# The first group of a fused dynamic-convolution and gated-MLP kernel: its down products taken in three fp32r parts instead of one float32 product

## The chip, the cores and the metric

One core of one Trainium2 chip. The time is the device time of one execution in microseconds (us); the kernel before was run three times, and its median is 1341.92 us (1340.8 to 1342.03). In the profile, PE is TensorE's matmul, PEld its weight load, DVE is VectorE, ACT ScalarE, POOL GpSimd, SP the queue that issues the DMAs.

## What is computed

```python
w = softmax(weight_gen, axis=-1)                # [4, 4096, 8, 7]
x = sum over k of w[:, s, h, k] * x_pad[:, s + k, h, :]   # causal, 7 taps, [4, 4096, 192]
x = x.reshape(16384, 192)
g = x @ w_gate                                  # [16384, 1536]
silu = g * (1 / (1 + exp(-g)))
out = (silu * (x @ w_val)) @ w_out              # [16384, 192]
```

x and weight_gen are float32, the three matrices are float64 in memory; the result is float32.

## The kernel before, in words

The 16384 tokens are worked in 32 groups g of 512 (JG = 4 tiles of 128). For each group the hidden width of 1536 is worked in 12 steps f of 128, so there are 384 steps, numbered i = 12 g + f. A value is held as a pair: hi is the value rounded to fp32r, lo the rest, and a product a b is taken as three fp32r products, hi hi, lo hi and hi lo.

A step of TensorE has three kinds of work. `up_first` (L440 for the left 64 rows of the width, L443) and `up_second` (L452) take the products with w_gate and w_val into two PSUM banks, in halves of 64 rows; four banks rotate, so the banks of step i are needed again at step i + 2 and come free when DVE has read them. `down` (L497, L504, L513) multiplies the gated value of the step two before (LAG = 2) with w_out and sums over f. Between the two halves of a sum stands a marker: `told` puts an empty instruction into POOL's queue that waits for the first half, and `behind` lets the second half wait for this instruction. So TensorE's `up_second` waits until POOL's queue has come as far as the marker of its step (the releaser is shown as POOLq L281).

After `up_second`, ACT takes `silu` of the gate (sg, L460), and `gated` multiplies it with the value on DVE. In groups 1 to 31 this gives h (L474), its rounded part hi on ACT (L475), then one other piece of DVE work, then lo (L477). In group 0 (PLAIN = 1) all other pieces of the step come first, and then one product, hi, in plain float32 (L469); it has no lo.

The weights come as float64 and are made float32 while group 0 runs. For each f four pieces (`weight_ops`) do this: `exponent` (DVE e L363, ACT Relu L372 and Sign L374, POOL sign L375), `mantissa_high` (DVE m L380), `mantissa_low` (DVE m L390), and `value32` (DVE w L403, then the splits of the first two matrices: hi on ACT L353, lo on POOL L354). Step i of group 0 holds value32 of f = i + 2, mantissa_high of i + 3, exponent of i + 4 and mantissa_low of i + 3, in this order, and behind them pieces of the softmax and of the convolution of group 1 (DVE prod L231, xatt L261; three products aside on POOL, L231). The part of w_out is copied into a float32 tile `wo32` (ACT L417), which the down product of group 0 reads in float32 (L497). In steps 9 to 13 (WO = 9) the twelve parts of `wo32` are split into `wo` hi and lo (ACT L353, POOL L354), for groups 1 to 31.

Every engine works its instructions in the order in which this program writes them.

Of the kernel before, what the change touches and what calls it, by code (L numbers as in the profile page):

```python
# [8 lines left out]
F32 = mybir.dt.float32  # L9
F32R = mybir.dt.float32r  # L10
I32 = mybir.dt.int32
AF = mybir.ActivationFunctionType
ALU = mybir.AluOpType
# [5 lines left out]
def dynconv_glu_kernel(  # L19
# [23 lines left out]
    nc = tc.nc  # L43
    B, S, D = x.shape
# [3 lines left out]
    P = 128  # L48
# [6 lines left out]
    NF = F // P  # L55

    LAG = 2
# [1 line left out]
    LEAD1 = 1  # L59
    EXP1 = 16  # L60
    LOAD1 = 1
    WO = 9

    PLAIN = 1

    HELPED = (3, 3)
    ASIDE = max(HELPED)
# [6 lines left out]
    const = ctx.enter_context(tc.tile_pool(name="const", bufs=1))  # L74
# [15 lines left out]
    wb_hi = const.tile([P, F], F32R, name="wb_hi")  # L90
    wb_lo = const.tile([P, F], F32R, name="wb_lo")
    wo = const.tile([P, NF, 2, D], F32R, name="wo")
    wo32 = const.tile([P, NF, D], F32, name="wo32")

    xr = x.rearrange("b (q t) d -> (b q) t d", t=T)
    wgr = weight_gen.rearrange("b (q t) h k -> (b q) t (h k)", t=T)
# [182 lines left out]
    def told(ins):  # L279

        nop = nc.gpsimd.nop()  # L281
        tc.add_manual_dep(nop.ins, ins.ins.name, SYNC, reason="the sum's other half")
        return nop
# [51 lines left out]
    NW = 3 * P + D  # L335
    raw_t = {}

    def load_weights(f):
        raw = stage.tile([P, NW, 2], I32, tag="raw", name="raw", bufs=RAW)
        fs = slice(f * P, (f + 1) * P)  # L340
        pieces = (
            (raw[:, 0:P], w_gate[0:P, fs]),
            (raw[:, P : 2 * P], w_val[0:P, fs]),
            (raw[0:DB, 2 * P : 3 * P], w_gate[P:D, fs]),
            (raw[DB:P, 2 * P : 3 * P], w_val[P:D, fs]),
            (raw[:, 3 * P : NW], w_out[fs]),
        )
        for dst, src in pieces:
            nc.sync.dma_start(out=dst.rearrange("p n w -> p (n w)"), in_=src.bitcast(I32))  # L349
        raw_t[f] = raw  # L350

    def split(hi, lo, src):
        nc.scalar.activation(out=hi, in_=src, func=AF.Copy)  # L353
        nc.gpsimd.tensor_tensor(out=lo, in0=src, in1=hi.bitcast(F32), op=ALU.subtract)  # L354

    def weight_ops(f):
        st = {}
        fs = slice(f * P, (f + 1) * P)

        def exponent():  # L360
            raw = st["raw"] = raw_t.pop(f)
            e = stage.tile([P, NW], I32, tag="e", name="e")
            nc.vector.tensor_scalar(  # L363
                out=e,
                in0=raw[:, :, 1],
                scalar1=20,
                scalar2=0x7FF,
                op0=ALU.logical_shift_right,
                op1=ALU.bitwise_and,
            )  # L370

            nc.scalar.activation(out=e, in_=e, func=AF.Relu, scale=TWO23, bias=exp_bias)  # L372
            sign = stage.tile([P, NW], F32, tag="sign", name="sign")
            nc.scalar.activation(out=sign, in_=raw[:, :, 1], func=AF.Sign)  # L374
            nc.gpsimd.tensor_tensor(out=sign, in0=sign, in1=e.bitcast(F32), op=ALU.mult)  # L375
            st["scale"] = sign

        def mantissa_high():
            st["m"] = stage.tile([P, NW], I32, tag="m", name="m")
            nc.vector.tensor_scalar(  # L380
                out=st["m"],
                in0=st["raw"][:, :, 1],
                scalar1=0xFFFFF,
                scalar2=4,
                op0=ALU.bitwise_and,
                op1=ALU.logical_shift_left,
            )

        def mantissa_low():
            nc.vector.scalar_tensor_tensor(  # L390
                out=st["m"],
                in0=st["raw"][:, :, 0],
                scalar=28,
                in1=st["m"],
                op0=ALU.logical_shift_right,
                op1=ALU.bitwise_or,
            )
            if f + RAW < NF:
                load_weights(f + RAW)

        def value32():
            w = stage.tile([P, NW], F32, tag="w", name="w")
            nc.vector.scalar_tensor_tensor(  # L403
                out=w,
                in0=st["m"],
                scalar=float(2**24),
                in1=st["scale"],
                op0=ALU.add,
                op1=ALU.mult,
            )  # L410
            split(wb_hi[:, fs], wb_lo[:, fs], w[:, 2 * P : 3 * P])
            split(
                wa_hi[:, :, fs],
                wa_lo[:, :, fs],
                w[:, 0 : 2 * P].rearrange("p (i n) -> p i n", i=2),
            )
            nc.scalar.activation(out=wo32[:, f], in_=w[:, 3 * P : NW], func=AF.Copy)  # L417

        return [exponent, mantissa_high, mantissa_low, value32]


    h_t = {}
    acc = {}
# [38 lines left out]

    def gated(g, f, sums, sg, between):
        hi = hp.tile([P, NC], F32R, tag="hi", name="hi", bufs=KEEP)
        if g < PLAIN:
            while between():
                pass
            h = hi.bitcast(F32)
            nc.vector.tensor_tensor(out=h, in0=sums[1], in1=sg, op=ALU.mult)  # L469
            h_t[g, f] = h, None  # L470
            return
        h = hp.tile([P, NC], F32, tag="h", name="h")
        lo = hp.tile([P, NC], F32R, tag="lo", name="lo", bufs=KEEP)
        nc.vector.tensor_tensor(out=h, in0=sums[1], in1=sg, op=ALU.mult)  # L474
        nc.scalar.activation(out=hi, in_=h, func=AF.Copy)  # L475
        between()
        nc.vector.tensor_tensor(out=lo, in0=h, in1=hi.bitcast(F32), op=ALU.subtract)  # L477
        h_t[g, f] = hi, lo
# [5 lines left out]
    def down(g, f, pair, second):  # L484


        hi, lo = h_t[g, f]
        opens, closes = f == 0 and not second, f == NF - 1 and second
        ts = (2 * pair, 2 * pair + 1)
        if opens:  # L490
            for t in ts:
                acc[t] = ps_dn.tile([P, 2 * D], F32, tag=f"dn{t}", name=f"dn{t}")
        order = ts if (f + second) % 2 == 0 else ts[::-1]
        tiles = [(t, r, slice(t * P, (t + 1) * P)) for t, r in zip(order, (LOW, HIGH))]
        if lo is None:
            made = [
                nc.tensor.matmul(  # L497
                    acc[t][:, 0:D], hi[r, cs], wo32[r, f], start=opens, stop=closes
                )
                for t, r, cs in tiles  # L500
            ]
        else:
            made = [
                nc.tensor.matmul(  # L504
                    acc[t],
                    hi[r, cs],
                    wo[r, f].rearrange("p a d -> p (a d)"),
                    start=opens,
                    stop=False,
                )  # L510
                for t, r, cs in tiles
            ] + [
                nc.tensor.matmul(  # L513
                    acc[t][:, 0:D], lo[r, cs], wo[r, f, 0], start=False, stop=closes
                )
                for t, r, cs in tiles
            ]
        if not second:
            half_done[pair] = told(made[-1])
            return  # L520
        behind(made[0], half_done.pop(pair))
        if f < NF - 1:
            return
        if pair == 0:
            osb_t[g] = outp.tile([P, JG, 2 * D], F32, tag="osb", name="osb", bufs=1)
        osb = osb_t[g]
        n = D if lo is None else 2 * D
        for t in ts:
            nc.scalar.activation(out=osb[:, t, 0:n], in_=acc[t][:, 0:n], func=AF.Copy)
        if g < NG - 1 and pair == 0:  # L530
            return
        t0, t1 = (ts[0] if g == NG - 1 else 0), ts[1] + 1
        if lo is not None:
            a = osb[:, t0:t1]
            nc.vector.tensor_tensor(
                out=a[:, :, 0:D], in0=a[:, :, 0:D], in1=a[:, :, D:], op=ALU.add
            )
        nc.sync.dma_start(
            out=outr[:, g * JG + t0 : g * JG + t1], in_=osb[:, t0:t1, 0:D]
        )  # L540
# [6 lines left out]
    def spread(ops, first, last):  # L547

        for n, op in enumerate(ops):
            at = first + (n * (last - first)) // len(ops)  # L550
            todo.setdefault(max(at, 0), []).append(op)

    with tc.manual_schedule():
# [31 lines left out]
        for i in range(NF):  # L585
# [4 lines left out]
        todo[0] += later[:3]  # L590
        spread(loads, LOAD1, LOAD1 + 7)
        spread(later[3:], NF - LEAD - 2, NF - LEAD)
        spread(
            [lambda f=f: split(wo[:, f, 0], wo[:, f, 1], wo32[:, f]) for f in range(NF)],
            WO,
            NF + LAG - 1,
        )
        for c in range(1, len(wcuts)):
            s0 = (wcuts[c - 1][0] // JG - 1) * NF - LEAD if c > 1 else NF
            s1 = (wcuts[c][0] // JG - 1) * NF - LEAD  # L600
# [18 lines left out]
        for i in range(len(steps) + LAG + 1):  # L619
            ops = todo.pop(i, [])  # L620
            to_turn = turned.get(i)
            if i < len(steps):
                g, f = steps[i]
                sums, nop = up_first(g, f)
# [19 lines left out]
            if i < len(steps):  # L644
                up_second(g, f, sums, nop)
                sg = silu(sums)
# [6 lines left out]
            if i < len(steps):  # L653

                def between():
                    if ops:
                        ops.pop(0)()
                    return ops
# [40 lines left out]
```

## Time and profile before

| | |
|---|---|
| median of three runs | 1341.92 us |
| the profiled execution | 1342.55 us, span of its instructions 1340.8 us |
| TensorE busy | 1287.4 us, 96% |
| DVE busy | 1010.5 us, 75% |
| ACT busy | 608.5 us, 45% |
| POOL busy | 71.8 us, 5%, all of it before 108 us |
| mean granted clock of TensorE | 0.991 |

The span runs from the first to the last instruction. Busy time of an engine counts its instructions, not its waits; a matmul's end is modelled. Group 0 lasts from the first up product at 30.78 us to about 103 us.

### The profile page before, as it was taken

To read this page: it belongs to the slowest core of one execution; us is meant where nothing else is said; L and a number is where in the kernel's file an instruction comes from. 1 tells how busy PE (TensorE), PEld (TensorE's weight loads), DVE (VectorE), ACT (ScalarE), POOL (GpSimd) and SP (SyncE) were. 2 spreads that over 40 slices of the span, in tenths; PEclk is the share of its full clock that TensorE was granted. 3 is DMA by queue.
4 is the path that set the end of the run, shared out by engine and by line. 5 is a ranking of instruction groups with operands and counts; after the bars stand their busy time and mean duration, and the time that the engine had idled before them with its cause. 6 is when DMAs were issued, how large, how long until landed. Compare 5 with 4: busy or idle time off the path is not lost.

```text
span 1340.8 us, 31630 instructions
## 1 busy us (share of the span) xinstructions
PE 1287.4 (96%) x13560; PEld 1205.6 (90%) x13560; DVE 1010.5 (75%) x1385; ACT 608.5 (45%) x1073; POOL 71.8 (5%) x66
## 2 busy tenths in 40 slices
PE   1689999999999999999999999999999999999998
PEld 0578999999999999999999999999999999999998
DVE  8988787777877777887777788777778777777753
ACT  3445444454444445444444544444454444444443
POOL 6761000000000000000000000000000000000000
PEclk9879999999999999999999999999999999999999
DMA  5421100101110010110101011010101001000000
GB/s 152 140 75 34 55 13 13 43 13 55 33 55 13 2 55 13 54 34 23 41 4 55 13 54 31 13 43 13 55 13 55 14 1 54 13 13 13 13 14 13
DMA packets 28580, 47.36 MB, mean 35 GB/s; under 512 B 2076, under 2 KB 25628, under 8 KB 26648
## 3 DMA queue, kind: packets, MB, share of 16 engines
q1 hardware_dynamic: 28440, 45.34, 10.5%
q8 instruction: 106, 1.74, 0.5%
q14 instruction: 34, 0.28, 0.1%
HBM read 32.75 MB, written 12.58 MB: 34 GB/s over the span
## 4 chain that ended last, share of the span: by engine, by line
PE 88%; DVE 5%; ACT 3%; DMA 2%; issue 1%; SPq 1%; POOL 0%; ACTq 0%; DVEq 0%; POOLq 0%
PE dn L504 22%; PE up L440 21%; PE up L452 20%; PE up L443 18%; PE dn L513 5%; PE tr L300 1%; DVE h L474 1%; DMA xt<-in_x_dram 1%; SPq L349 1%; ACT sg L460 1%; DVE xatt L261 1%; DMA raw<-in_moe_w_gate_dram 1%; DVE m L390 1%; ACT wt L183 0%; ACT L460 0%
## 5 line engine op out<-in xcount | busy, mean ns | idle before, releaser
L504 PE MATMUL dn<-wo,hi 64*128 64x384 f32 x2976 | 599.6, 346 | 0.4 <-ACT hi L475 0.4
L513 PE MATMUL dn<-wo,lo 64*128 64x192 f32 x2976 | 531.7, 248 | 0.3 <-DVE lo L477 0.3
L504 PEld LDWEIGHTS dn<-wo,hi 64*128 64x128 f32 x2976 | 476.2, 184 | 19.0 <-ACT hi L475 0.6
L513 PEld LDWEIGHTS dn<-wo,lo 64*128 64x128 f32 x2976 | 443.3, 186 | 9.0 <-DVE lo L477 0.5
L474 DVE TENSOR_TENSOR h<-up,sg 128x512 f32<-128x512 f32 x372 | 256.8, 690 | 240.4 <-ACT sg L460 240.3
L460 ACT ACTIVATE sg<-up 128x512 f32<-128x512 f32 x384 | 229.4, 597 | 381.3 <-PE up L452 347.0
L475 ACT ACTIVATE hi<-h 128x512 fp32r<-128x512 f32 x372 | 235.2, 632 | 298.1 <-DVE h L474 298.1
L477 DVE TENSOR_TENSOR lo<-h,hi 128x512 fp32r<-128x512 f32 x372 | 255.5, 687 | 73.2 <-ACT hi L475 73.2
L440 PE MATMUL up<-xhi,wb_hi 64*128 64x512 f32 x768 | 242.4, 424 | 5.3 <-DVE hi L469 3.4
L452 PE MATMUL up<-xhi,wa_hi 64*128 64x512 f32 x768 | 234.2, 426 | 11.5 <-POOLq L281 11.4
L440 PE MATMUL up<-xlo,wb_hi 64*128 64x512 f32 x768 | 229.2, 394 | 0.9 <-DVE xlo L325 0.9
L440 PE MATMUL up<-xhi,wb_lo 64*128 64x512 f32 x768 | 229.0, 395 | 0.0
L443 PE MATMUL up<-xhi,wa_hi 64*128 64x512 f32 x768 | 227.6, 392 | 0.0
L443 PE MATMUL up<-xhi,wa_lo 64*128 64x512 f32 x768 | 227.6, 392 | 0.0
L443 PE MATMUL up<-xlo,wa_hi 64*128 64x512 f32 x768 | 226.7, 390 | 0.0
L452 PE MATMUL up<-xhi,wa_lo 64*128 64x512 f32 x768 | 220.3, 392 | 0.0
L452 PE MATMUL up<-xlo,wa_hi 64*128 64x512 f32 x768 | 219.5, 390 | 0.0
L231 DVE TENSOR_TENSOR prod<-xt,wt 128x768 f32<-128x768 f32 x186 | 181.9, 978 | 0.2
L261 DVE TENSOR_TENSOR xatt<-xatt,prod 128x768 f32<-128x768 f32 x186 | 179.1, 963 | 0.0
L440 PEld LDWEIGHTS up<-xhi,wb_hi 64*128 64x128 f32 x768 | 136.9, 185 | 11.6 <-DVE hi L469 4.5
L443 PEld LDWEIGHTS up<-xhi,wa_hi 64*128 64x128 f32 x768 | 137.0, 186 | 9.3
L443 PEld LDWEIGHTS up<-xhi,wa_lo 64*128 64x128 f32 x768 | 136.6, 185 | 9.1
(57 smaller groups left out, 1354.6 us busy)
## 6 DMA issues: line engine op xcount, KB each, us to landing
xt<-in_x_dram SPq DMA_DIRECT2D x14, 1344.0 KB, 5.6
out_dram<-osb SPq DMA_DIRECT2D x31, 384.0 KB, 2.6
raw<-in_moe_w_out_dram SPq DMA_DIRECT2D x12, 192.0 KB, 2.8
wt<-in_weight_gen_dram SPq DMA_DIRECT2D x3, 672.0 KB, 4.0
raw<-in_moe_w_gate_dram SPq DMA_DIRECT2D x12, 128.0 KB, 2.1
raw<-in_moe_w_val_dram SPq DMA_DIRECT2D x12, 128.0 KB, 2.3
wt<-in_weight_gen_dram SPq DMA_DIRECT2D x4, 224.0 KB, 4.4
xt<-in_x_dram SPq DMA_DIRECT2D x2, 384.0 KB, 4.5
```

The costliest lines, as they stand in the source:

```text
L231: engine.tensor_tensor(out=into.rearrange("p t (h i) -> p t h i", h=H), in0=src, in1=w, op=ALU.mult)
L261: nc.vector.tensor_tensor(out=a, in0=a, in1=tmp.pop(k), op=ALU.add)
L300: nc.tensor.transpose(ps[half][:, t * P + r.start : t * P + r.stop], xatt[g][r, t, half * P : (half + 1) * P], ident[r, r],)
L440: nc.tensor.matmul(ps, w[r, fs], m[r], start=(n == 0), stop=False)
L443: ins = nc.tensor.matmul(sums[i], w[r, i, fs], m[r], start=False, stop=False)
L452: ins = nc.tensor.matmul(sums[i], w[r, i, fs], m[r], start=False, stop=(n == len(full) - 1))
L460: nc.scalar.activation(out=sg, in_=sums[0], func=AF.Silu)
L474: nc.vector.tensor_tensor(out=h, in0=sums[1], in1=sg, op=ALU.mult)
L475: nc.scalar.activation(out=hi, in_=h, func=AF.Copy)
L477: nc.vector.tensor_tensor(out=lo, in0=h, in1=hi.bitcast(F32), op=ALU.subtract)
L504: nc.tensor.matmul(acc[t], hi[r, cs], wo[r, f].rearrange("p a d -> p (a d)"), start=opens, stop=False,)
L513: nc.tensor.matmul(acc[t][:, 0:D], lo[r, cs], wo[r, f, 0], start=False, stop=closes)
```

## The change

PLAIN is gone: group 0 takes the same way as the others, with h, hi and lo, and three down products. `value32` splits its part of w_out at once into `wo` hi and lo; the tile `wo32` and the twelve later splits are gone. The closing addition of the two halves of a sum is now done for group 0 too.

```diff
-            nc.scalar.activation(out=wo32[:, f], in_=w[:, 3 * P : NW], func=AF.Copy)
+            split(wo[:, f, 0], wo[:, f, 1], w[:, 3 * P : NW])
...
     def gated(g, f, sums, sg, between):
         hi = hp.tile([P, NC], F32R, tag="hi", name="hi", bufs=KEEP)
-        if g < PLAIN:
-            while between():
-                pass
-            h = hi.bitcast(F32)
-            nc.vector.tensor_tensor(out=h, in0=sums[1], in1=sg, op=ALU.mult)
-            h_t[g, f] = h, None
-            return
         h = hp.tile([P, NC], F32, tag="h", name="h")
...
-        if lo is None:
-            made = [
-                nc.tensor.matmul(
-                    acc[t][:, 0:D], hi[r, cs], wo32[r, f], start=opens, stop=closes
-                )
-                for t, r, cs in tiles
-            ]
-        else:
-            made = [
...
-        spread(
-            [lambda f=f: split(wo[:, f, 0], wo[:, f, 1], wo32[:, f]) for f in range(NF)],
-            WO,
-            NF + LAG - 1,
-        )
```

DVE, steps 1 and 2 of the program, the kernel before (e and the first m are the pieces of the exponent and the high mantissa, the second m the low one, w the float32 weight, hi the gated product of the step):

```order
L403 SCALAR_TENSOR_TENSOR w<-m,sign 128x576
L380 TENSOR_SCALAR m<-raw 128x576
L363 TENSOR_SCALAR e<-raw 128x576
L390 SCALAR_TENSOR_TENSOR m<-raw,m 128x576
L231 TENSOR_TENSOR prod<-xt,wt 128x768
L469 TENSOR_TENSOR hi<-up,sg 128x512
L403 SCALAR_TENSOR_TENSOR w<-m,sign 128x576
L380 TENSOR_SCALAR m<-raw 128x576
L363 TENSOR_SCALAR e<-raw 128x576
L390 SCALAR_TENSOR_TENSOR m<-raw,m 128x576
L261 TENSOR_TENSOR xatt<-xatt,prod 128x4x192
L469 TENSOR_TENSOR hi<-up,sg 128x512
```

and the same two steps of the changed kernel:

```order
L463 TENSOR_TENSOR h<-up,sg 128x512
L399 SCALAR_TENSOR_TENSOR w<-m,sign 128x576
L466 TENSOR_TENSOR lo<-h,hi 128x512
L376 TENSOR_SCALAR m<-raw 128x576
L359 TENSOR_SCALAR e<-raw 128x576
L386 SCALAR_TENSOR_TENSOR m<-raw,m 128x576
L227 TENSOR_TENSOR prod<-xt,wt 128x768
L463 TENSOR_TENSOR h<-up,sg 128x512
L399 SCALAR_TENSOR_TENSOR w<-m,sign 128x576
L466 TENSOR_TENSOR lo<-h,hi 128x512
```

The gated product has moved from the end of its step to its head, and lo stands between w and the masks.

ACT, step 1, before:

```order
L460 ACTIVATE sg<-up 128x512
L353 ACTIVATE wb_hi<-w 128x128
L353 ACTIVATE wa_hi<-w 128x2x128
L417 ACTIVATE wo_93<-w 128x192
L372 ACTIVATE e<-e,exp_bias 128x576
L374 ACTIVATE sign<-raw 128x576
```

and now:

```order
L456 ACTIVATE sg<-up 128x512
L464 ACTIVATE hi<-h 128x512
L349 ACTIVATE wb_hi<-w 128x128
L349 ACTIVATE wa_hi<-w 128x2x128
L349 ACTIVATE wo<-w 128x192
L368 ACTIVATE e<-e,exp_bias 128x576
L370 ACTIVATE sign<-raw 128x576
```

The rounding of h stands between the Silu and the conversions; the copy of w_out's part is the first half of its split now.

POOL, steps 1 and 2, before (sign is the product of sign and scale):

```order
L354 TENSOR_TENSOR wb_lo<-w,wb_hi 128x128
L354 TENSOR_TENSOR wa_lo<-w,wa_hi 128x2x128
L375 TENSOR_TENSOR sign<-sign,e 128x576
L354 TENSOR_TENSOR wb_lo<-w,wb_hi 128x128
L354 TENSOR_TENSOR wa_lo<-w,wa_hi 128x2x128
L375 TENSOR_TENSOR sign<-sign,e 128x576
L231 TENSOR_TENSOR aside<-xt,wt 128x768
```

and now:

```order
L350 TENSOR_TENSOR wb_lo<-w,wb_hi 128x128
L350 TENSOR_TENSOR wa_lo<-w,wa_hi 128x2x128
L350 TENSOR_TENSOR wo<-w,wo 128x192
L371 TENSOR_TENSOR sign<-sign,e 128x576
L350 TENSOR_TENSOR wb_lo<-w,wb_hi 128x128
L350 TENSOR_TENSOR wa_lo<-w,wa_hi 128x2x128
L350 TENSOR_TENSOR wo<-w,wo 128x192
L371 TENSOR_TENSOR sign<-sign,e 128x576
L227 TENSOR_TENSOR aside<-xt,wt 128x768
```

Each step has a third split, ahead of the sign product and the marker behind it.

## Rows read from the trace of the kernel before

**Rows 1.** The page of the profile: busy time of each engine with its share and instructions; then, over the span in 40 slices, the busy share of DVE and TensorE's granted clock, in tenths.
```profile
PE 1287.4 (96%) x13560; PEld 1205.6 (90%) x13560; DVE 1010.5 (75%) x1385; ACT 608.5 (45%) x1073; POOL 71.8 (5%) x66
DVE  8988787777877777887777788777778777777753
PEclk9879999999999999999999999999999999999999
```

**Rows 2.** Busy time by stage: the stretch, its length, then for PE, PEld, DVE, ACT and POOL the busy us and the instructions in brackets, TensorE's granted clock, the share of the DMA engines, GB/s.
```profile
45.00:50.00 5.00, 1.67 (x8) 1.39 (x10) 5.00 (x5) 1.39 (x2) 4.89 (x4) 0.68 0.19 57
50.00:55.00 5.00, 5.00 (x36) 4.39 (x36) 5.00 (x7) 2.80 (x6) 3.68 (x4) 0.64 0.83 273
55.00:60.00 5.00, 3.26 (x34) 2.68 (x34) 5.00 (x5) 2.74 (x6) 3.95 (x5) 1.00 0.35 108
60.00:65.00 5.00, 3.93 (x38) 3.25 (x40) 5.00 (x7) 2.79 (x6) 3.85 (x4) 1.00 0.57 163
...
95.00:100.00 5.00, 5.00 (x54) 4.76 (x52) 4.03 (x5) 2.67 (x8) 3.54 (x4) 1.00 0.00 0
```

**Rows 3.** Timeline of DVE: start in us, duration in us, engine, line, operation, out<-in and shapes, count, and in square brackets the idle time before it and what ended it.
```profile
32.35 0.45 DVE L380 TENSOR_SCALAR m<-raw 128x576 int32<-128x576 int32 x1
...
35.13 0.76 DVE L403 SCALAR_TENSOR_TENSOR w<-m,sign 128x576 f32<-128x576 int32 x1 [1.30 <-POOL sign L375]
...
41.63 0.68 DVE L469 TENSOR_TENSOR hi<-up,sg 128x512 f32<-128x512 f32 x1
...
57.48 0.71 DVE L363 TENSOR_SCALAR e<-raw 128x576 int32<-128x576 int32 x1
...
60.18 0.68 DVE L469 TENSOR_TENSOR hi<-up,sg 128x512 f32<-128x512 f32 x1
60.78 1.38 DVE L403 SCALAR_TENSOR_TENSOR w<-m,sign 128x576 f32<-128x576 int32 x1
62.08 0.45 DVE L380 TENSOR_SCALAR m<-raw 128x576 int32<-128x576 int32 x1
62.45 0.45 DVE L363 TENSOR_SCALAR e<-raw 128x576 int32<-128x576 int32 x1
...
77.37 0.74 DVE L403 SCALAR_TENSOR_TENSOR w<-m,sign 128x576 f32<-128x576 int32 x1
78.04 1.68 DVE L380 TENSOR_SCALAR m<-raw 128x576 int32<-128x576 int32 x1
...
87.14 0.68 DVE L469 TENSOR_TENSOR hi<-up,sg 128x512 f32<-128x512 f32 x1
...
90.67 0.69 DVE L469 TENSOR_TENSOR hi<-up,sg 128x512 f32<-128x512 f32 x1 [0.45 <-ACT sg L460]
```

**Rows 4.** Timeline of POOL, the same columns.
```profile
59.82 1.73 POOL L375 TENSOR_TENSOR sign<-sign,e 128x576 f32<-128x576 f32 x1 [1.05 <-ACT sign L374]
62.58 0.63 POOL L354 TENSOR_TENSOR wb_lo<-w,wb_hi 128x128 fp32r<-128x128 f32 x1 [1.04 <-PE up L443]
63.18 1.24 POOL L354 TENSOR_TENSOR wa_lo<-w,wa_hi 128x256 fp32r<-128x256 f32 x1
...
92.88 1.70 POOL L354 TENSOR_TENSOR wo<-wo,wo 128x192 fp32r<-128x192 f32 x3
```

**Rows 5.** Timeline of TensorE (matmuls), the same columns: the second parts of four steps of group 0, its first and third pair, and of two steps of group 1.
```profile
48.33 0.79 PE L452 MATMUL up<-xhi,wa_hi 64*128 64x512 f32 x2 [3.99 <-POOLq L281]
...
49.34 0.63 PE L452 MATMUL up<-xhi,wa_lo 64*128 64x512 f32 x2
...
59.88 0.50 PE L452 MATMUL up<-xhi,wa_hi 64*128 64x512 f32 x2 [1.74 <-POOLq L281]
...
60.44 0.40 PE L452 MATMUL up<-xhi,wa_lo 64*128 64x512 f32 x2
...
97.64 0.53 PE L452 MATMUL up<-xhi,wa_hi 64*128 64x512 f32 x1
...
101.00 0.52 PE L452 MATMUL up<-xhi,wa_hi 64*128 64x512 f32 x1
...
152.02 0.41 PE L452 MATMUL up<-xhi,wa_hi 64*128 64x512 f32 x1
...
155.22 0.41 PE L452 MATMUL up<-xhi,wa_hi 64*128 64x512 f32 x1
```

**Rows 6.** Timeline of ACT, the same columns: the Silu of steps 0 and 4, and the two instructions that lead to POOL's sign product.
```profile
36.76 0.60 ACT L460 ACTIVATE sg<-up 128x512 f32<-128x512 f32 x1 [3.42 <-PE up L452]
...
58.28 0.77 ACT L372 ACTIVATE e<-e,exp_bias 128x576 int32<-128x576 int32 x1 [1.38 <-DVE e L363]
58.97 0.70 ACT L374 ACTIVATE sign<-raw 128x576 f32<-128x576 int32 x1
60.94 0.60 ACT L460 ACTIVATE sg<-up 128x512 f32<-128x512 f32 x1 [1.27 <-PE up L452]
```

**Rows 7.** Groups of instructions from 0 to 140 us: line, engine, operation, out<-in, shapes, count | busy us, mean ns of one | idle before in us and what ended it.
```profile
L354 POOL TENSOR_TENSOR wo<-wo,wo 128x192 fp32r<-128x192 f32 x12 | 9.2, 795 | 5.0 <-PE dn L497 3.1 <-ACT wo L353 1.9
L477 DVE TENSOR_TENSOR lo<-h,hi 128x512 fp32r<-128x512 f32 x11 | 7.5, 686 | 1.4 <-ACT hi L475 1.4
```

**Rows 8.** Waits of TensorE from 30 to 130 us: who waited for whom, us in total, times, the longest.
```profile
PE up L452 <- POOLq L281: 11.4, 7, 4.0
PE up L440 <- DVE hi L469: 3.4, 3, 1.8
```

More of the change, by code (lines that the diff above doesn't have):

```diff
@@ L61, in dynconv_glu_kernel @@
     LOAD1 = 1
-    WO = 9
-    PLAIN = 1
     HELPED = (3, 3)
@@ L92, in dynconv_glu_kernel @@
     wo = const.tile([P, NF, 2, D], F32R, name="wo")
-    wo32 = const.tile([P, NF, D], F32, name="wo32")
     xr = x.rearrange("b (q t) d -> (b q) t d", t=T)
@@ L494, in down @@
         tiles = [(t, r, slice(t * P, (t + 1) * P)) for t, r in zip(order, (LOW, HIGH))]
-        if lo is None:
-            made = [
-                nc.tensor.matmul(
-                    acc[t][:, 0:D], hi[r, cs], wo32[r, f], start=opens, stop=closes
-                )
-                for t, r, cs in tiles
-            ]
-        else:
-            made = [
[L504 to L509, printed above, removed]
-                )
[L511 to L517, printed above, removed]
+        made = [
+            nc.tensor.matmul(
+                acc[t],
+                hi[r, cs],
+                wo[r, f].rearrange("p a d -> p (a d)"),
+                start=opens,
+                stop=False,
+            )
+            for t, r, cs in tiles
+        ] + [
+            nc.tensor.matmul(
+                acc[t][:, 0:D], lo[r, cs], wo[r, f, 0], start=False, stop=closes
+            )
+            for t, r, cs in tiles
+        ]
         if not second:
@@ L526, in down @@
         osb = osb_t[g]
-        n = D if lo is None else 2 * D
         for t in ts:
-            nc.scalar.activation(out=osb[:, t, 0:n], in_=acc[t][:, 0:n], func=AF.Copy)
+            nc.scalar.activation(out=osb[:, t], in_=acc[t], func=AF.Copy)
         if g < NG - 1 and pair == 0:
@@ L532, in down @@
         t0, t1 = (ts[0] if g == NG - 1 else 0), ts[1] + 1
[L533 to L537, printed above, removed]
+        a = osb[:, t0:t1]
+        nc.vector.tensor_tensor(out=a[:, :, 0:D], in0=a[:, :, 0:D], in1=a[:, :, D:], op=ALU.add)
         nc.sync.dma_start(
@@ L592, in dynconv_glu_kernel @@
         spread(later[3:], NF - LEAD - 2, NF - LEAD)
-        spread(
-            [lambda f=f: split(wo[:, f, 0], wo[:, f, 1], wo32[:, f]) for f in range(NF)],
-            WO,
-            NF + LAG - 1,
-        )
         for c in range(1, len(wcuts)):
```

## The prediction, made before the changed kernel was run

> **What bounds the kernel now.** I read the shares of busy time first, then a table by stage, then the timelines of each engine in the first 125 us. TensorE is busy for 96% of the span and its clock is full except in the first three of the forty slices, so after the start-up TensorE sets the time. In the first slices DVE is the busy engine [rows 1]. The table by stage shows where the one hands over to the other: from 45 to 65 us DVE works 5.00 of every 5 us and TensorE 1.67 to 5.00, at a granted clock of 0.68 and 0.64 in the two stretches after 45 us; by 95 us DVE is at 4.03 and TensorE at 5.00 [rows 2]. The change touches only this first group (steps f = 0 to 11, 35 to about 103 us), so whatever it moves there shifts all that follows: behind it TensorE has no slack to take a delay back.
>
> Inside the group the rows show three things. First, DVE's stream: hi of f = 0 starts at 41.63 and of f = 8 at 87.14, that is 5.69 us a step, without an idle entry [rows 3]. Second, what releases TensorE: its second part of a step waits for a marker in POOL's queue, and starts just after POOL's sign product has *started* (59.82, then 59.88), not after it ends (61.55) [rows 4, 5]. POOL's sign product starts when ACT's Sign is done (58.97 + 0.70 = 59.67). So the loop that feeds TensorE runs over ACT's Sign, not over POOL's throughput. Third, DVE and POOL exclude each other: w took 0.74 with POOL idle (77.37) and 1.38 beside sign, ending 0.61 after it (62.16 against 61.55); the integer mask m took 0.45 alone (62.08) and 1.68 beside sign (78.04) [rows 3, 4].
>
> **The change, part by part.**
>
> *h first, then the conversions.* Before, DVE does all of a step's conversions and takes the product at the end; ACT and TensorE run up to a step ahead. Now h heads the step's work on DVE, and h waits for the Silu of the same step. What is queued behind the waiting h is w, the masks and e, the operand of the Relu and Sign that let TensorE start the next step. A loop closes that was open before.
>
> At step 0 this costs a delay of its own. xlo ends where m starts, at 32.35, and sg of step 0 ends at 36.76 + 0.60 = 37.36. Before, DVE did 41.63 - 32.35 - 1.30 (its one idle stretch, before the w of 35.13) = 7.98 us of work up to hi. Now this work comes after h and beside lo: 37.36 + 0.05 + 0.60 (h) + 0.69 (lo) + 7.98 = 46.7 us, where h of f = 1 can start [rows 3, 5, 6].
>
> For steps 1 to 7, which each carry an e, I go round the loop from one Silu to the next. Silu 0.60 (60.94); h 0.60 (the distance from hi at 60.18 to w at 60.78); w 0.67 (77.37 to 78.04); lo 0.69; m and e 0.37 each (62.08 to 62.45); hand-over 0.09 (57.48 + 0.71 to 58.28); Relu 0.69 (58.28 to 58.97); Sign 0.70; to POOL's start 0.15, to TensorE 0.06; the three pairs 0.96 (59.88 to 60.44 + 0.40); hand-over 0.10. Sum 6.05 us [rows 3 to 7]. Behind e DVE has only the low mantissa and a piece or two of about 1 us left, less than the 3.3 us that the loop still needs from there. That is the least, with POOL never in the way. But POOL is: its splits start 0.42 after w ends (62.16 to 62.58) and last 0.63 and 1.24, so m slips in at the end of wb_lo, 1.05 after w, and e only behind wa_lo, 1.05 + 0.37 + 1.24 = 2.66, where it would start at 1.06 unhindered. The stall is 0 to 1.6; I take 0.75. w costs 1.30 instead of 0.67 beside an aside, which three of these steps have or follow: 0.25 on average (bounds 0 and 0.63). lo waits for a POOL operation in progress for 0 to 0.57 (one wo split, 1.70 / 3): 0.25. So 6.05 + 1.25 = **7.3 us a step**, bounds 6.05 and 8.85. f = 8 starts its h at 46.7 + 7 x 7.3 = 97.8 where hi stood at 87.14: **+10.7 us**.
>
> *lo and the split of w_out, step 8.* Step 8 carries no e, so DVE's own stream decides: lo 0.69 and, if DVE has to wait it out, the wo split 0.57 on POOL: **+1.2** (bounds 0.7 and 1.2). From f = 9 on DVE already waited for the others (0.45 at 90.67), and the lo of f = 9 to 11 lie under TensorE: nothing. If that cover were gone, 3 x 0.69 = 2.1.
>
> *TensorE's clock.* After a wait of 3.99 us the three pairs of the second part took 49.34 + 0.63 - 48.33 = 1.64 us instead of 0.96, and the granted clock of the stretch was 0.68; after waits of 1.74 it was 1.00 [rows 2, 5]. In a loop of 7.3 us with 3.4 us of matmuls (the step that TensorE needs in full clock, below) the wait would be about 3.9 us. That is a price of 0.68 for a step that runs at the lower level, in the loop itself. But a step at the lower level also doubles TensorE's other work and so leaves a wait of less than 1 us before the next, and behind short waits the rows show the full clock. I take half of the seven steps: **+2.4** (bounds 0 and 4.8). [...]
>
> *TensorE's products.* Two float32 products per tile become hi (384 columns) and lo (192). A step that TensorE sets took 101.00 - 97.64 = 3.36 us with the float32 form and takes 155.22 - 152.02 = 3.20 with the three products [rows 5]. Some four steps (f = 10 to the last of the group's sums) are set by TensorE: 4 x 0.16 = **-0.6**. Before that the gain lies inside the wait for POOL.
>
> *What is removed late.* The twelve splits in steps 9 to 13 (POOL 9.2 us, and ACT's halves) leave [rows 7]. From 95 to 100 us DVE is not full and TensorE idles for 0.00 of 5 us [rows 2], so there is nothing to give back: I cost it at nothing. ACT's copy into the float32 tile becomes the hi split of the same size: no difference. The wo tile is read two steps after its split, later than its lo half by far: no wait. There is no DMA in the change.
>
> **The sum.** 10.7 + 1.2 + 2.4 - 0.6 = 13.7 us on top of the profiled execution's 1342.55 (span 1340.8) gives 1356.25. That execution is 0.63 above the median of the runs, 1341.92, so the forecast for the median is **1355.6 us**. With the low bounds (6.05 a step, 0.7, 0, -0.6) h of f = 8 is at 89.1, +1.9, and the sum +2.0: 1343.9. With all high bounds (8.85, 1.2, 4.8) it is +26.9: 1368.8.
>
> **The rivals.**
>
> *Faster: h first frees TensorE.* TensorE waited 3.4 us for hi to give back its PSUM banks [rows 8], once for 1.8 us. With h at the head of the step the banks come back early, and the low clock behind these waits goes too. At most that is 3.4 plus about 3 us for each of the two stretches at half clock behind them: about 9.4, 1332.5 us. It decides if the loop is shorter than the 5.69 us a step of before. Against it: even without a stall the loop sums to 6.05. Chance 0.05.
>
> *Every step at the low clock.* The price is 0.68 in all seven steps, sum 16.1, 1358.0 us. For it: the two stretches after the 3.99 us wait were at 0.68 and 0.64. Against it: the full clock of 55 to 60 us, where TensorE was at work for 3.26 of 5 us [rows 2]. [...] Chance 0.20.
>
> *No change.* TensorE's 96% covers the group's work, only the -0.6 remains: 1341.3 us. For it, that lo and wo are short and spread over twelve steps. Against it, DVE without an idle entry from 41.63 to 90.67: it has no room for eight lo. Chance 0.06.
>
> *Full blocking.* Every w, lo, m and e meets a POOL operation: the loop is 8.85, h of f = 8 at 108.7, and with 1.2 and -0.6 and no clock term the sum is +22.1, 1364.0 us. For it: w and m each show a full wait for sign [rows 3]. Against it: from 45 to 65 us POOL stands idle for 3.6 of 20 us, and at the head of a step, while DVE waits for the Silu, sign can run out without hurting it [rows 2]. Chance 0.09.
>
> **How the numbers follow.** My forecast has 0.60, the rivals 0.05, 0.20, 0.06 and 0.09. A measurement of this kernel can tell about 0.2%, 2.7 us, from no change. Faster is the first rival, 0.05; same is the third, 0.06; slower is the rest, 0.89. The range of the forecast's own terms, 1344 to 1369, holds less likely ends on both sides, since all bounds would have to fall together; I set 1346 to 1364, which holds the clock rival and half of the blocking one and leaves out the faster case, the no-change case and the tails.
>
> **What would show it.** In the changed kernel's profile h of the first group should wait for ACT's sg at nearly each of steps 1 to 8, and DVE should have idle time between 45 and 95 us. h of f = 1 should start near 47 us, of f = 8 near 98. The waits of TensorE's second part for POOL's queue should grow from 11 us to over 20. The distance of the Silus from step 1 to 8 should be 7 to 8 us. From f = 10 on, steps of 3.2 us. DVE's total should grow by 8 us, POOL's stay. It is wrong if h finds sg ready at each step and DVE stays full (then the throughput of DVE alone counts, about 8 x 1.3), if the step is near 6 us, or if the shift at f = 8 is not found again at the end of the run.

## The result and the profile after

The changed kernel takes **1360.85 us** (median of 4 runs, 1360.11 to 1361.39) against 1341.36 us before (4 runs): ratio 1.0142, 95% interval 1.0129 to 1.0155, +19.5 us. The forecast was 1355.6 (1346 to 1364), slower. The profiled execution took 1361.03 us with a span of 1359.2, that is +18.4 in span; the steps below are worked out against that.

The page of the changed kernel: busy time by engine, then DVE's busy share and TensorE's granted clock in the 40 slices, then the two groups that answer to the loop, with what ended the idle time before them.

```profile
PE 1288.2 (95%) x13560; PEld 1210.0 (89%) x13560; DVE 1017.7 (75%) x1398; ACT 614.6 (45%) x1073; POOL 65.4 (5%) x66
DVE  7779877778777777877777787777778777777743
PEclk9779999999999999999999999999999999999999
L463 DVE TENSOR_TENSOR h<-up,sg 128x512 f32<-128x512 f32 x384 | 264.9, 690 | 255.9 <-ACT sg L456 255.8
L448 PE MATMUL up<-xhi,wa_hi 64*128 64x512 f32 x768 | 233.7, 427 | 31.1 <-POOLq L277 31.0
```

DVE was at 8 to 9 tenths in the first four slices [rows 1]; now it is at 7, 7, 7, 9, and TensorE's clock is at 7 and 7 tenths in the second and third slice, where it was at 8 and 7. By stage, in the columns of [rows 2]; the last row is the second part of step 7 alone:

```profile
55.00:60.00 5.00, 5.00 (x34) 4.21 (x32) 3.17 (x5) 2.10 (x5) 2.42 (x3) 0.55 0.81 264
60.00:65.00 5.00, 3.08 (x24) 2.42 (x22) 2.86 (x4) 2.00 (x3) 3.52 (x4) 0.79 0.36 99
...
93.73:95.38 1.65, 1.65 (x8) 1.37 (x10) 0.24 (x1) 0.00 (x0) 1.51 (x1) 0.50 0.00 0
```

DVE, full here before, works 3.17 and 2.86 of 5 us from 55 to 65. From 60 to 65 no engine is full: that is how a closed loop looks. (From 55 to 60 TensorE is at work throughout, but at a granted clock of 0.55.) DVE's timeline, columns as in [rows 3]: step 0, then the turn from step 6 to 7 up to e, then the end of step 7.

```profile
36.69 0.69 DVE L463 TENSOR_TENSOR h<-up,sg 128x512 f32<-128x512 f32 x1 [4.73 <-ACT sg L456]
...
40.95 1.66 DVE L359 TENSOR_SCALAR e<-raw 128x576 int32<-128x576 int32 x1
...
45.02 2.05 DVE L227 TENSOR_TENSOR xatt<-xt,wt 128x768 f32<-128x768 f32 x1
46.99 2.30 DVE L227 TENSOR_TENSOR prod<-xt,wt 128x768 f32<-128x768 f32 x1
49.21 0.68 DVE L463 TENSOR_TENSOR h<-up,sg 128x512 f32<-128x512 f32 x1
...
88.42 0.69 DVE L463 TENSOR_TENSOR h<-up,sg 128x512 f32<-128x512 f32 x1 [2.14 <-ACT sg L456]
89.03 0.75 DVE L399 SCALAR_TENSOR_TENSOR w<-m,sign 128x576 f32<-128x576 int32 x1
89.81 0.69 DVE L466 TENSOR_TENSOR lo<-h,hi 128x512 fp32r<-128x512 f32 x1
...
91.05 0.98 DVE L359 TENSOR_SCALAR e<-raw 128x576 int32<-128x576 int32 x1
...
101.61 2.00 DVE L257 TENSOR_TENSOR xatt<-xatt,aside 128x768 f32<-128x768 f32 x1
104.57 0.69 DVE L463 TENSOR_TENSOR h<-up,sg 128x512 f32<-128x512 f32 x1 [0.97 <-ACT sg L456]
```

The same stretches on ACT (the first row is the Silu of step 1), then on POOL:

```profile
46.79 0.60 ACT L456 ACTIVATE sg<-up 128x512 f32<-128x512 f32 x1 [2.68 <-PE up L448]
...
87.79 0.60 ACT L456 ACTIVATE sg<-up 128x512 f32<-128x512 f32 x1 [1.95 <-PE up L448]
...
92.13 0.78 ACT L368 ACTIVATE e<-e,exp_bias 128x576 int32<-128x576 int32 x1 [1.45 <-DVE e L359]
92.82 0.71 ACT L370 ACTIVATE sign<-raw 128x576 f32<-128x576 int32 x1
95.48 0.60 ACT L456 ACTIVATE sg<-up 128x512 f32<-128x512 f32 x1 [1.96 <-PE up L448]
...
103.64 0.42 ACT L260 ACTIVATE xatt<-xatt 128x256 f32<-128x256 f32 x1 [2.42 <-DVE xatt L257]
103.96 0.58 ACT L456 ACTIVATE sg<-up 128x512 f32<-128x512 f32 x1
```

```profile
40.77 1.53 POOL L371 TENSOR_TENSOR sign<-sign,e 128x576 f32<-128x576 f32 x1 [6.36 <-ACT sign L370]
...
44.64 1.61 POOL L371 TENSOR_TENSOR sign<-sign,e 128x576 f32<-128x576 f32 x1
46.22 2.26 POOL L227 TENSOR_TENSOR aside<-xt,wt 128x768 f32<-128x768 f32 x1
...
90.78 0.94 POOL L350 TENSOR_TENSOR wa_lo<-w,wa_hi 128x256 fp32r<-128x256 f32 x1
...
93.67 1.57 POOL L371 TENSOR_TENSOR sign<-sign,e 128x576 f32<-128x576 f32 x1 [1.19 <-ACT sign L370]
...
101.36 1.43 POOL L371 TENSOR_TENSOR sign<-sign,e 128x576 f32<-128x576 f32 x1 [1.18 <-ACT sign L370]
```

And TensorE's second parts, as in [rows 5]: steps 1, 2, 6, 7 (first and third pair), 8 (the same), 11 and 12.

```profile
45.10 0.80 PE L448 MATMUL up<-xhi,wa_hi 64*128 64x512 f32 x2 [7.69 <-POOLq L277]
...
54.49 0.80 PE L448 MATMUL up<-xhi,wa_hi 64*128 64x512 f32 x2 [4.90 <-POOLq L277]
...
86.04 0.80 PE L448 MATMUL up<-xhi,wa_hi 64*128 64x512 f32 x2 [4.68 <-POOLq L277]
...
93.73 0.79 PE L448 MATMUL up<-xhi,wa_hi 64*128 64x512 f32 x2 [2.32 <-POOLq L277]
...
94.75 0.63 PE L448 MATMUL up<-xhi,wa_lo 64*128 64x512 f32 x2
...
101.42 0.50 PE L448 MATMUL up<-xhi,wa_hi 64*128 64x512 f32 x2 [2.71 <-POOLq L277]
...
101.97 0.40 PE L448 MATMUL up<-xhi,wa_lo 64*128 64x512 f32 x2
...
116.15 0.42 PE L448 MATMUL up<-xhi,wa_hi 64*128 64x512 f32 x2
119.36 0.41 PE L448 MATMUL up<-xhi,wa_hi 64*128 64x512 f32 x2
```

One turn can be read off: Silu at 87.79, h at 88.42, w, lo, m, e to 92.03, Relu, Sign to 93.53, POOL's sign at 93.67, TensorE at 93.73, the next Silu at 95.48: 7.69 us. The step that TensorE starts at 101.00 before [rows 5] starts at 119.36: +18.36, the whole difference in span. By the Silus the distance falls to 17.5 in steps 13 to 15 and is back at 18.4 from step 16 on, up to the end: all the loss lies in the first group.

### The profile page after: what moved, and what is told of

Same layout as the page of the kernel before. It is cut to its first block, busy times and chain, and to the rows that moved or that the text cites. A ratio compares the mean times of both kernels' runs of the same rounds, so it can differ in the third digit from the quotient of the medians.

```text
span 1359.2 us, 31634 instructions
## 1 busy us (share of the span) xinstructions
PE 1288.2 (95%) x13560; PEld 1210.0 (89%) x13560; DVE 1017.7 (75%) x1398; ACT 614.6 (45%) x1073; POOL 65.4 (5%) x66
## 4 chain that ended last, share of the span: by engine, by line
PE 87%; DVE 5%; ACT 3%; issue 1%; SPq 1%; DMA 1%; ACTq 0%; POOL 0%; DVEq 0%; POOLq 0%
PE dn L485 22%; PE up L448 21%; PE up L436 20%; PE up L439 18%; PE dn L494 6%; DVE h L463 1%; PE tr L296 1%; ACT sg L456 1%; SPq L345 1%; DVE xatt L257 1%; DVE e L359 1%; ACT hi L464 1%; DVE m L386 0%; DMA xt<-in_x_dram 0%; ACT wt L179 0%
## 5 line engine op out<-in xcount | busy, mean ns | idle before, releaser
L485 PE MATMUL dn<-wo,hi 64*128 64x384 f32 x3072 | 616.6, 347 | 0.4 <-ACT hi L464 0.4
L494 PE MATMUL dn<-wo,lo 64*128 64x192 f32 x3072 | 543.7, 249 | 0.3 <-DVE lo L466 0.3
L485 PEld LDWEIGHTS dn<-wo,hi 64*128 64x128 f32 x3072 | 484.7, 185 | 19.2 <-ACT hi L464 0.6
L494 PEld LDWEIGHTS dn<-wo,lo 64*128 64x128 f32 x3072 | 452.2, 187 | 9.8 <-DVE lo L466 0.5
L463 DVE TENSOR_TENSOR h<-up,sg 128x512 f32<-128x512 f32 x384 | 264.9, 690 | 255.9 <-ACT sg L456 255.8
L464 ACT ACTIVATE hi<-h 128x512 fp32r<-128x512 f32 x384 | 242.8, 632 | 311.2 <-DVE h L463 311.2
L466 DVE TENSOR_TENSOR lo<-h,hi 128x512 fp32r<-128x512 f32 x384 | 263.5, 686 | 73.1 <-ACT hi L464 72.9
L448 PEld LDWEIGHTS up<-xhi,wa_hi 64*128 64x128 f32 x768 | 130.3, 186 | 34.0 <-POOLq L277 34.0
L439 PEld LDWEIGHTS up<-xhi,wa_hi 64*128 64x128 f32 x768 | 135.8, 186 | 9.1
```

The source lines that it names most:

```text
L439: ins = nc.tensor.matmul(sums[i], w[r, i, fs], m[r], start=False, stop=False)
L448: ins = nc.tensor.matmul(sums[i], w[r, i, fs], m[r], start=False, stop=(n == len(full) - 1))
L485: nc.tensor.matmul(acc[t], hi[r, cs], wo[r, f].rearrange("p a d -> p (a d)"), start=opens, stop=False,)
L494: nc.tensor.matmul(acc[t][:, 0:D], lo[r, cs], wo[r, f, 0], start=False, stop=closes)
```

## The experiments

All runs are timed beside the kernel before on the same chip (medians 1340.9 to 1341.9). The intervals of the ratios are some 0.15% to either side, 2 us; 1.3 us where there were nine or ten runs. A difference between two of the experiments is less sure than either: an estimate from these intervals is 2.7 us to either side. "The marker" is the one in POOL's queue that TensorE's second part waits for.

**e1_h_late**: the order of before, all added work kept.

```
+                while g == 0 and len(ops) > 1:   # ahead of gated()
+                    ops.pop(0)()
```

> The changed kernel with one thing undone: in group 0 all pieces of a step but one come before h, then h, the rounding on ACT, the last piece, lo. All added work stays. Closed loop (h waits for the Silu at the head of the step, and e, which lets TensorE go on, stands behind it): the loop opens again and only the added work is left, per step lo 0.69 and at most 0.57 for the split of w_out, in eight steps 5 to 10 us over the kernel before: 1347 to 1351 us. Added work (DVE and POOL have more to do in a full stretch, in whatever order): stays at 1360.9, within 1.5.

Measured: 1349.6, ratio 1.0059 (1.0044 to 1.0074). DVE is full again (10.0 of 10 us from 50 to 80) and the step is 6.70 us (h from 40.69 to 94.32 in eight). So, by these two medians, the order costs 11.2 of the 19.5, the added work 8.3.

**e2_plain_h_first**: the kernel before, only the order changed, float32 product kept.

```
-            while between():
-                pass
```

> The kernel before with the order alone changed: in group 0 the float32 product h stands at the head of its step, with all other pieces behind it; no lo, no early split, the float32 down product. Closed loop: a step goes from 5.7 us to about 7.91 - 0.69 = 7.2, h of step 8 stands near 99 us instead of 87, the time is 1350 to 1355 us. Added work: nothing is added, so 1341.4 within 1.5.

Measured: 1350.84, ratio 1.0064 (1.0049 to 1.0079). The order alone costs 9.9 us, in the range; the product waits for the Silu for 17.2 us in group 0 (17.5 in the changed kernel), and TensorE waits for the marker for 22.8. But the product of step 8, expected near 99 us, came at 92.10, 5.0 later than before:

```profile
92.10 0.69 DVE L467 TENSOR_TENSOR hi<-up,sg 128x512 f32<-128x512 f32 x1 [0.97 <-ACT sg L460]
```

From step 1 to 8 a turn takes 6.26 us (48.27 to 92.10 in seven), not 7.2. Another 3.5 came in steps 9 and 10 (the product of step 10 at 104.44, before 96.01), which was not forecast and whose cause was not followed. So that the order costs is shown here; that all 9.9 us are the loop's turns is not.

**e3_e_first**: the changed kernel with e ahead of h in steps 1 to 7.

```
+                if g == 0 and 1 <= f < NF - 4:
+                    ops.pop(2)()
```

> The changed kernel with the exponent piece (e) of steps 1 to 7 ahead of h, and a third buffer for the tiles of e and sign so that it can run there; the work is the same. Closed loop: w, lo, m and the waits for POOL leave the loop; it would be near 6 us, and DVE's own work, 5.7 + 1.26 = 6.95 us a step, sets the time: 7 x (7.9 - 6.95) = 6.7 us less, 1354 us; at most 13 us less, 1347. Added work: 1360.9 within 1.5.

Measured: 1360.83, ratio 1.0144 (1.0127 to 1.016): missed, nothing gained. The loop is open (in steps 1 to 7 h waits for no Silu), but ACT's hi now stands behind Relu and Sign, and lo waits for it and then meets POOL's operations. DVE, ACT and POOL of this kernel in step 6:

```profile
89.42 0.74 DVE L399 SCALAR_TENSOR_TENSOR w<-m,sign 128x576 f32<-128x576 int32 x1
90.94 1.54 DVE L466 TENSOR_TENSOR lo<-h,hi 128x512 fp32r<-128x512 f32 x1 [0.79 <-ACT hi L464]
...
90.30 0.61 ACT L464 ACTIVATE hi<-h 128x512 fp32r<-128x512 f32 x1
...
90.54 1.40 POOL L371 TENSOR_TENSOR sign<-sign,e 128x576 f32<-128x576 f32 x1 [2.83 <-ACT sign L370]
```

lo took 1.54 instead of 0.69 and came 0.79 late. I had not followed what else stands in ACT's queue.

**e7_e_first_lo_last**: e3 with lo at the end of steps 1 to 7.

```
+        while g == 0 and 1 <= f < NF - 4 and between():   # between h and lo
+            pass
```

> e3_e_first (1360.8) with lo at the end of steps 1 to 7 instead of right behind h. If e3_e_first gained nothing because lo waited 0.77 us a step for ACT's hi, which there stands behind Relu and Sign: 5.4 less, 1355, and to 1351 if lo then also misses POOL's operations. If DVE's stream is as long however it is ordered, because POOL's operations block it for their length: 1360.8, within 1.5.

Measured: 1356.24, ratio 1.0109 (1.0094 to 1.0124), 4.6 less than e3: the reason given for e3's miss holds. DVE is full (9.9 of 10 us). With lo out of the way, opening the loop is worth these 4.6 us, step 0 as it was.

**e11_step0_late**: the changed kernel with the pieces of step 0 alone ahead of h.

```
+                while i == 0 and len(ops) > 1:
+                    ops.pop(0)()
```

> The changed kernel (1360.9) with the pieces of step 0 alone ahead of h, steps 1 to 11 as they are. If step 0 costs a delay of its own (its second part started 4.1 us later than before at step 1): 4 less, about 1357. If the loop of steps 1 to 8 takes up whatever step 0 gives (DVE has as much work before h of step 1 either way): 1360.9, within 1.5.

Measured: 1355.96, ratio 1.0111 (1.0097 to 1.0124): 4.9 less. The second part of step 1 starts at 40.19 instead of 45.10. Step 0 costs a delay of its own; with e7's 4.6 it makes 9.5 of the 11.2 us of the order, if the two add up; no run has both. The rest, 1.7, is less than two runs can tell apart.

**e12_sign_dve**: the changed kernel; from tile 4 on DVE makes the product of sign and exponent in the next step.

```
-            nc.gpsimd.tensor_tensor(out=sign, in0=sign, in1=e.bitcast(F32), op=ALU.mult)
+            st["pair"] = sign, e
+            if f < 4:
+                nc.gpsimd.tensor_tensor(out=sign, in0=sign, in1=e.bitcast(F32), op=ALU.mult)
...
+            nc.vector.tensor_tensor(out=sign, in0=sign, in1=e.bitcast(F32), op=ALU.mult)  # behind m
```

> The changed kernel (1360.9), h first as it is, but from tile 4 on the product of sign and exponent is made by DVE in the next step, so that the marker in POOL's queue no longer stands behind ACT's Sign. Theory of the closed loop over Sign: the loop is open, h waits for no Silu, the step is DVE's own stream, 6.5 to 7.4 us with the added product, in place of 7.9: 4 to 11 less, 1350 to 1357. If h first costs only by what DVE does: the product adds 0.75 x 7, 1366.

Measured: 1356.6, ratio 1.0114 (1.01 to 1.0128): 4.25 less, in the range, although DVE got more work. But "h waits for no Silu" was wrong: it waits for 0.47 to 0.49 us in four of steps 1 to 7, and these turns take 6.69 to 6.71 us. ACT's timeline here, step 4 to 5, then TensorE's second part of step 5 and POOL's last split:

```profile
68.34 0.58 ACT L462 ACTIVATE sg<-up 128x512 f32<-128x512 f32 x1
...
70.87 0.34 ACT L349 ACTIVATE wo<-w 128x192 fp32r<-128x192 f32 x1
73.75 0.78 ACT L368 ACTIVATE e<-e,exp_bias 128x576 int32<-128x576 int32 x1 [2.53 <-DVE e L359]
74.43 0.71 ACT L370 ACTIVATE sign<-raw 128x576 f32<-128x576 int32 x1
75.04 0.57 ACT L462 ACTIVATE sg<-up 128x512 f32<-128x512 f32 x1
...
71.33 0.50 PE L454 MATMUL up<-xhi,wa_hi 64*128 64x512 f32 x2 [3.22 <-POOLq L277]
...
71.90 0.40 PE L454 MATMUL up<-xhi,wa_lo 64*128 64x512 f32 x2
...
72.22 1.11 POOL L350 TENSOR_TENSOR wo<-w,wo 128x192 fp32r<-128x192 f32 x1
```

TensorE had its second part done by 72.3 (71.90 + 0.40), yet the Silu starts at 75.04: it stands in ACT's queue behind Relu and Sign, which wait for e. The loop closes a second time there, at 6.70 us a turn from Silu to Silu. (In other turns DVE's own work comes last: the h of step 5 follows its xatt without a wait at 77.45.) So the loop of the prediction had two ways round, over the marker and over ACT's own order, the former the longer by the marker and the matmuls.

**e5_filled**: the changed kernel with idle TensorE filled.

```
+                            for _ in range(16):   # two matmuls of 128 columns each, not read; ahead of the second part
```

> The changed kernel (1360.9) with 16 extra pairs of 128-column matmuls on TensorE in each of seven steps of the first group, into unused columns of the accumulators, so that TensorE does not stand idle while it waits for POOL. What they write isn't read. Clock theory (a part of the loss is that six of the eight second parts run for 1.31 to 1.65 us instead of 0.96): all seven at about 0.96, 7.0 us a step, some 4 us less, 1357. Closed loop without a part of the clock: 1360.9, within 1. If the extra matmuls themselves hold up the next step, slower than 1361.

Measured: 1359.29, ratio 1.0129 (1.0114 to 1.0145): 1.6 less, a miss of the 4 expected. The edit fills steps 3 to 8 only, six and not seven. The second parts of steps 3, 5, 6 and 7 took 0.96 (there 1.31, 0.96, 1.65, 1.65: 1.7 saved); that of step 4 stayed at 1.65 although filled, that of step 2 was not filled and stayed too. That a step at the low clock goes into the time one to one fits these numbers, but the two intervals overlap, so it is not shown. How to keep the clock in all steps was not found.

**e4_no_wo_lo** and **e8_h_late_no_wo_lo**: the changed kernel, and e1, without POOL's split of w_out (the low half of w_out is zero).

```
-            split(wo[:, f, 0], wo[:, f, 1], w[:, 3 * P : NW])
+            nc.scalar.activation(out=wo[:, f, 0], in_=w[:, 3 * P : NW], func=AF.Copy)
```

> The changed kernel without POOL's lo split of w_out: the lo half is set to zero once at the start, so one of the three products adds nothing. Closed loop: in POOL's queue the split stands behind wb_lo and wa_lo, and e slips in before it; only the low mantissa waits for it, outside the loop: 0 to 2 us less, 1359 to 1361. If the exclusion of DVE by the added POOL split is what costs: nine times 0.57 to 0.8, 1354 to 1356.

> e1_h_late (1349.6: the changed kernel with h at the end of the step) without POOL's split of w_out; the low half of w_out is zero. It parts the added work. If lo of h on DVE alone makes the 8.6 us over the kernel before (8 x 0.69 = 5.5, the rest clock): 1347 to 1349.6. If POOL's split costs DVE its whole length (8 x 0.57 = 4.6): about 1345.

Measured: 1357.23, ratio 1.0114 (1.0099 to 1.0129), 3.6 less than the changed kernel, between the two expectations; and 1345.11, ratio 1.0026 (1.0016 to 1.0035), 4.5 less than e1. Where DVE sets the time, the split costs 4.5 us in all, as much as eight times its unhindered length (8 x 0.57, from 1.70 / 3 [rows 4]). It does not come evenly: 1.6 lie before h of f = 0 (40.69 in e1, 39.05 here) and 2.5 in the eight steps behind it (to 94.32 and 90.17). What is left over the kernel before, 3.2 us, is lo with all that goes with it.

**e6_no_aside1**: the kernel before, group 1's three products on DVE.

```
-    HELPED = (3, 3)
+    HELPED = (3, 0)
```

> The kernel before (1341), with the second set's three products of the first group back on DVE where POOL had them. Theory that DVE and POOL exclude each other (a product of 1.9 us on POOL holds DVE up for its whole length, on DVE itself it takes 0.87): 3 x 1.0 less, about 1338. Theory that only DVE's own busy time counts: 3 x 0.87 more, about 1343.6.

Measured: 1341.65, ratio 0.9998 (0.9989 to 1.0008): no difference. Within 1.3 us, what DVE no longer loses to POOL and what it does itself weigh the same.

**e9_lows_dve** and **e10_lows_sign_dve**: the kernel before with the low splits of w_gate and w_val on DVE behind e, and then the sign product too.

```
-            for f, part in ((i + 2, 3), (i + 3, 1), (i + 4, 0), (i + 3, 2)):
+            for f, part in ((i + 2, 3), (i + 3, 1), (i + 4, 0), (i + 2, 4), (i + 3, 2)):   # 4: both lows; e10: (i + 3, 5), the product, ahead of (i + 4, 0)
```

> The kernel before (1341.5), with the two low splits of each tile of w_gate and w_val (POOL: 0.63 and 1.24 us) made by DVE behind e, from tile 2 on. DVE gets some 0.65 us a step (two subtractions, by the rate of lo, 0.69 for 512 columns). If POOL's operations cost DVE their whole length wherever they stand, as e8_h_late_no_wo_lo showed of the split of w_out: 8 x (0.65 - 1.87) = -10, about 1332. If they cost it the share that the trace of before gives over the whole stretch (DVE's operations are 15.5 us longer than their shortest, POOL works for 36.7 us, so 0.42 of it): 8 x (0.65 - 0.79) = -1, no difference that can be told. If DVE's own stream alone counts: +5, 1346.5.

> e9_lows_dve, and from tile 4 on the product of sign and exponent on DVE too, a step later, so that POOL keeps the asides alone. Whole length: a further 7 x (0.75 - 1.9) = -8, some 1324. Share of 0.42: 7 x (0.75 - 0.8), the same time as e9_lows_dve. DVE's own stream alone: +5 over e9_lows_dve.

Measured: 1346.51, ratio 1.0038 (1.0025 to 1.005), and 1344.54, ratio 1.0026 (1.0016 to 1.0036): both slower, so my whole-length price does not carry over as a total. The 1346.5 of "DVE's own stream alone" is e9's time, but by chance: DVE's stream got shorter and not 5 us longer, as its timeline in e9 shows.

```profile
38.15 1.47 DVE L426 TENSOR_TENSOR wb_lo<-w,wb_hi 128x128 fp32r<-128x128 f32 x1 [2.28 <-ACT wb_hi L419]
...
45.87 0.68 DVE L484 TENSOR_TENSOR hi<-up,sg 128x512 f32<-128x512 f32 x1
...
86.87 0.68 DVE L484 TENSOR_TENSOR hi<-up,sg 128x512 f32<-128x512 f32 x1
...
89.74 0.29 DVE L426 TENSOR_TENSOR wb_lo<-w,wb_hi 128x128 fp32r<-128x128 f32 x1 [1.52 <-ACT wb_hi L419]
...
100.11 0.69 DVE L484 TENSOR_TENSOR hi<-up,sg 128x512 f32<-128x512 f32 x1 [4.85 <-ACT sg L475]
```

From step 0 to 8 it is 4.5 us shorter than before (86.87 - 45.87 = 41.0, [rows 3] 45.5). But in step 0 and in step 9 DVE stands waiting for ACT's hi, and there the product comes 4.2 and the Silu of step 10 some 4 us later than before: the hi of step 9 starts at 92.53 (before 90.67), TensorE waits 2.56 us for it to give back its banks, and from 90 to 100 us its granted clock is 0.66. The new waits are mine, by placement. A version with the splits on DVE in steps 1 to 8 alone was not run; none of the runs beat the kernel before. That e10 comes within 2 us of e9 is what the share of 0.42 gave; whether that share is the right price stays open.

## Why the prediction was right, and where its size was off

The direction and the main mechanism hold: the loop over Silu, h, e, Sign and the marker closes, and its turn is what costs. The sum was short by 4.7 us (13.7 against 18.4 of the profiled executions). Two rivals, every step at the low clock (1358.0) and full blocking (1364.0), lie nearer to the 1360.85 than the 1355.6 does, but neither has the terms that were measured. Term by term:

- **Step 0: mis-sized, +2.5.** h of f = 1 was to start at 46.7 and started at 49.21. Its work was 3.2 us longer than forecast, and 0.7 of that was hidden by chance: h of f = 0 stands at 36.69 and not at 37.41, since this execution makes its first up product at 30.05 and that of before at 30.78; e6 and e9, where the start is that of before, have it at 29.92 and 30.02. The 7.98 us of work were taken from the trace of before as they stood there; now e (1.66) and xatt (2.05) meet two sign products and an aside on POOL, where they took 0.45 and 0.96 before. TensorE's clock has no part in it: the Silu of f = 1 was done at 47.39, and h stood behind prod (46.99 + 2.30). e11 shows that this term is real and about 4.9 us in all.
- **The turn, 7.3 us: right.** h of f = 1 to 8 took 55.36 us in seven turns, 7.91 each. Less the clock (3.1) and one other wait (1.5, next but one) it is 50.8, 7.25 a turn. The parts are less exact than the total: lo was held by POOL in none of the turns and w in one (1.50 at 80.72), where 0.25 a turn was forecast for each. And one turn, step 4 to 5, is not the loop's: h of f = 5 follows the low mantissa and two pieces of xatt without a wait, 4.1 us behind e (76.08 to 80.20), where the prediction had less than 3.3. In step 6 it is 3.00 us from w to the end of e, forecast 0.67 + 0.69 + 2 x 0.37 + 0.75 = 2.85; e (0.98) ends behind wa_lo's end at 91.72 (90.78 + 0.94).
- **TensorE's clock: 3.1 instead of 2.4.** Of the second parts of steps 2 to 8 four took 1.65 us (the granted clock of step 7's is 0.50) and one 1.31, two 0.96 and 0.95. The second rival (every step low) has 4.8; this trace does not show all seven low, and the truth lies between. Behind the two longest waits of these steps the part was low (4.90 before step 2, 4.68 before step 6). Behind shorter waits it has both cases: step 7 was low behind 2.32 us and step 8 was not behind 2.71. A length of wait from which the low clock follows is not shown; half of the steps was my estimate. That a low step doubles TensorE's other work is nearly so: at a granted clock of 0.50 the pairs of its first half follow each other by 0.43 us (57.42 to 57.85), at 1.00 by 0.23 (36.08 to 36.31). But the clock came back within step 6, and behind it TensorE waited 2.32 us and not less than 1.
- **ACT's queue before the Silu of step 8: not priced, +1.5.** TensorE was done at 102.37, but the Silu starts at 103.96, behind the copy of xatt, which waits for DVE's add (2.00, blocked by the sign product at 101.36). e3 and e12 fell to the same queue: what stands ahead of the Silu or hi on ACT belongs in the sum.
- **Step 8 and the late steps: right in sum.** From h of f = 8 to the step at 119.36 the shift grows by another 0.93 (18.36 - 17.43); the forecast for step 8 and two late steps is 1.2 - 0.3 = 0.9. A late step takes 3.21 us. The gain was counted for four steps and is left in two, +0.3 (what steps 13 to 15 gain, step 16 gives back).
- **The signs.** Found: DVE +7.2 (forecast 8), marker waits 31.0 us (over 20), late steps of 3.21, and h waiting for the Silu in six of steps 1 to 8 (not 1 and 5). Missed: h of f = 8 at 104.57 (near 98), and the Silus of steps 1 to 8 stand 8.2 us apart in the mean (7 to 8; h 7.9). POOL's total fell by 6.4 where none was forecast; nothing waits for that.

"Faster" and "no change" fell with the result; e1 and e2 show that the order costs. Full blocking gave 8.85 a turn; 7.25 excludes it.

One row was misread. The w of 77.37 was taken as one beside an idle POOL. POOL's timeline of before has a sign product there:

```profile
77.40 2.00 POOL L375 TENSOR_TENSOR sign<-sign,e 128x576 f32<-128x576 f32 x1
```

DVE came first, and it was POOL that was held (2.00 us; 1.43 at 101.36, where sign came first). The figure stands: w took 0.74 at 84.75 too, with POOL idle from 83.41 to 85.91.

## What to carry to other kernels

Before an operation is moved to the head of an in-order engine's step, write down what it waits for and what stands behind it, and go round: if an operand behind it leads back to what it waits for, the step becomes the sum of the turn, and engines that were full stand waiting, whatever the added work is. Look for every queue by which the turn can close (here POOL's marker and ACT's order), since opening one leaves the next. A stall moved into a start-up step costs once, but then in full: 4.9 us here.

## What the runs showed of the hardware

In these traces DVE and POOL block each other for whole operations, but not DVE's product, which reads one input from PSUM: it took 0.68 to 0.69 us in every row shown here, whatever POOL did; the hi of 60.18 ran inside the sign product of 59.82 [rows 3, 4]. Operations with all their inputs in SBUF were held: w took 1.38 beside sign (60.78 [rows 3]) and 0.74 alone (84.75), xatt 2.05 beside POOL's work and 0.95 alone (113.08 in the changed kernel), lo 1.54 in e3 and 0.68 alone (116.29 in the changed kernel). So were the masks m and e, which have one input: beside sign they took 1.68 (78.04 [rows 3]) and 1.66, elsewhere 0.45 (62.08 and 62.45 [rows 3]). Why the product is not held was not shown. What was new to me is that the price depends on the place: without POOL's split of w_out e8 gained 4.5 us, and with three of POOL's products moved to DVE e6 gained nothing, net of what DVE then does itself.

In e12 the marker passed before the operation ahead of it in POOL's queue had begun: TensorE starts at 71.33, 0.12 behind the end of ACT's hi of w_out that the last POOL split needs (70.87 + 0.34), while that split itself starts only at 72.22. In step 0 of the changed kernel it is the same: an aside stands ahead of the marker, its last operand is done at 44.98, TensorE starts at 45.10, the aside at 46.22. I read this as the marker passing when the operation ahead is *issued*, its operands being there. POOL's own durations are thus not in the turn by way of the marker, only its operands; by blocking e on DVE (0.98 at 91.05) they still are.
